# Sizes of the key and query weights from products of each weight chunk with itself on TensorE, and new instruction orders for the front of the kernel

## The chip, the cores and the metric

One core of a Trainium2 chip runs the whole kernel in one launch. The metric is the device time of one execution in microseconds (us); the kernel before took 1075.58 us, the median of 3 runs (1073.62 to 1076.91). Five engines work side by side, each in the order of its own instruction list, and wait for each other by semaphores: PE (TensorE, matrix products), DVE (VectorE), ACT (ScalarE), POOL (GpSimd) and SP (SyncE, which here only issues DMAs).

## The reference

The kernel is one transformer block with adaptive layer norm: linear attention with 32 heads, then a feed-forward layer with SiLU. There are 2048 tokens of width 576; the hidden width is 4608.

```python
mod = (_silu(c) @ w_mod).reshape(c.shape[0], 6, 1, -1)
sa, ca, ga, sb, cb, gb = (mod[:, 0], mod[:, 1], mod[:, 2], mod[:, 3], mod[:, 4], mod[:, 5])
h = _layernorm(x, axis=-1) * (1 + ca) + sa
x = x + ga * _A_ref(h, A_wqkv, A_wo)     # qkv = h @ wqkv; phi(t) = (t+1 if t>0 else exp(t)) + 1e-6
                                         # num = phi(q) @ (phi(k)^T v); den = phi(q) . sum phi(k); (num/den) @ wo
h = _layernorm(x, axis=-1) * (1 + cb) + sb
x = x + gb * _B_ref(h, B_w1, B_w2)       # silu(h @ w1) @ w2
```

Nothing in the reference is a norm of a weight. The norms are the kernel's own: it needs a power of two for each matrix that brings it into the range of 16-bit floats.

## The kernel before, in words

**Numbers.** TensorE multiplies 16-bit floats. Each 32-bit operand is scaled by a power of two and split into a high part (its value rounded to 16 bits) and a low part (the remainder); a product is three passes, high by high, low by high and high by low. The power of two for the key weights and for the query weights comes out of `find_size` (L514): from a bound of the matrix's norm it takes the square root's exponent by shifting the bits of the float (`scale_bits`, L511) and makes five small columns from it, SIZE, INV and the three of BY.

**How the work is tiled.** Tokens stand in 16 tiles of 128 rows, four tiles to a block. The width of 576 is cut in five chunks (START = 0..4): four of 128 and a tail of 64, which is loaded twice, into rows 0 to 63 and 64 to 127. The arrays `acc[0]` to `acc[15]`, 128 x 576 each, later hold the results; at the start they serve as landing places: `acc[0..4]` for the five chunks of the key weights, `acc[5..9]` for those of the query weights, `acc[12..15]` for the second block of x.

**The front of the kernel**, which the change touches, runs like this (the lines are those of the kernel before):

- SP issues the loads: two tiles of x, four full chunks and one tail of the modulation weights `w_mod` (`hT` and `tmod` in the profile), the key weights, two more tiles of x, the second block of x, the query weights.
- DVE and POOL normalise the first tiles (L367 to L384). ACT squares and sums the rows of `w_mod` (L626, L627). From their norm and that of the condition vector comes ETA, the power of two of the modulation (L628 to L639). DVE sums up four weighted chunks of `w_mod` (L645 to L654) and PE turns them into columns of shift and scale (`mod_col_of`, L563), which `add_cols` (L567) puts in `col_a`.
- **Key size.** For each key chunk DVE reduces the absolute maximum of every row (L641). The five maxima are squared and multiplied by 576 (L642), summed (L516), summed over the partitions by a product with a matrix of ones (L517), and turned into the scale (L518 to L527).
- With it the key weights are split: ACT makes the high parts (L500), DVE (L507) or POOL (L508, L509) the low parts.
- The first two tiles, turned by PE (L573), are modulated and split (L669, L392, L276), and PE multiplies them by the key weights into two banks of PSUM, `psK` (L590).
- **Query size.** ACT squares each query chunk with a sum over the row (L680, five times, each followed by a read of the accumulator). `find_size` then does the same as for the keys, and the query weights are split by L500, L507, L508, L509.
- `sigma_steps` (L968) makes the scale of the transformed keys. It uses the five maxima of the key size again: copied and multiplied in (L975, L977), reduced with two other rows (L978), summed by PE (L981), multiplied (L985).
- Then `phi` on each product: ACT takes the exponential (L530), DVE the linear part (L533) and the minimum with the sum (L542). The products with the query weights of tile 0 and 1 follow in the same two `psK` banks (L938), then keys and queries in turn for all tiles, and the sums over tokens of x^T phi(k) (L1087, `psG`).

`keep_busy` (L584) multiplies the matrix of ones by itself into a spare room, so that PE is never long without work in the front.

**After that** come the small matrices of all heads, the output projection (L420), the scales and first groups of the feed-forward layer (L1540, L1551), and from about 345 us to the end the feed-forward layer itself, which alternates products up (L2035) and down (L2119).

**What sets the order.** The instructions are first written in the order of the code and of a planner (tables STAGE_A and the class `Schedule`, the same before and after). At the end `arrange(ORDERS, begun)` lays a written permutation over the list of each engine: the table `ORDERS` names, by number, which instruction follows which. An engine never starts an instruction before the one ahead of it in that list.

## Time and profile before

| | |
|---|---|
| median of 3 runs | 1075.58 us (1073.62 to 1076.91) |
| the profiled execution | 1071.29 us |
| its span, first to last instruction | 1069.4 us |
| PE busy | 1042.4 us, 97% of the span |
| DVE busy | 901.8 us, 84% |
| ACT busy | 726.4 us, 68% |
| POOL busy | 753.2 us, 70% |
| mean granted clock of PE | 0.990 |

The profile is one execution. "Busy" counts an instruction from its start to its end, also while it is held up inside. A group's row gives the line, the engine, output and input, the shapes and the count, then busy us and the mean ns of one, then the idle time of the engine just before it and who ended it. A timeline row gives start, length, engine, line and operation. A product of two 32-bit operands has two records of PE in the timeline (x28 is 14 products). In the windows each row gives the length, the busy time and count of each engine, the granted clock of PE (1.00 is full speed), the DMA share and GB/s.

### The profile page before, as it was taken

The page shows a single profiled execution, that of the slowest core. Times are in us where ns is not written, and L with a number is a line of the kernel's source. Part 1 is how long each engine was busy: PE and PEld are TensorE (multiplying, and loading weights), DVE is VectorE, ACT ScalarE, POOL GpSimd, SP SyncE. Part 2 cuts the span into 40 slices and gives each one's busy share as a digit, 9 for nine tenths or more (in the row PEclk, how much of TensorE's full clock was granted, in tenths as well). Part 3 has the DMA queues.
Part 4 walks back from the last instruction along what each step waited for, and adds up shares of the span by engine and source line. Part 5 has one row for each costly group of instructions (what it writes and reads, how often), then busy time and mean ns, then how long its engine had stood idle before and what let it go on. Part 6 is the DMA issues. An engine that isn't in the chain of part 4 may idle for free.

```text
span 1069.4 us, 19132 instructions
## 1 busy us (share of the span) xinstructions
PE 1042.4 (97%) x6999; PEld 698.5 (65%) x6999; DVE 901.8 (84%) x1495; ACT 726.4 (68%) x1350; POOL 753.2 (70%) x818
## 2 busy tenths in 40 slices
PE   6889999999999999999999999999999999999998
PEld 5667778877776555666666666666666666666665
DVE  6998886698999999998988888977977987898767
ACT  5787585338667886776767767767767766676554
POOL 2586637466843888789798678876877778677563
PEclk7899999999999999999999999999999999999999
DMA  9299983096666877487667667667576667626423
GB/s 285 81 247 181 110 225 85 11 207 181 153 184 226 246 252 230 120 311 207 180 215 210 188 214 215 190 216 208 172 221 207 201 181 249 190 77 200 164 80 111
DMA packets 139245, 198.74 MB, mean 186 GB/s; under 512 B 63820, under 2 KB 96464, under 8 KB 139152
## 3 DMA queue, kind: packets, MB, share of 16 engines
q1 hardware_dynamic: 106340, 196.35, 61.5%
q10 hardware_dynamic: 32812, 1.18, 3.0%
q8 instruction: 54, 0.88, 0.3%
q14 instruction: 39, 0.32, 0.1%
HBM read 176.77 MB, written 15.48 MB: 180 GB/s over the span
## 4 chain that ended last, share of the span: by engine, by line
PE 81%; DVE 12%; DMA 3%; issue 1%; ACT 1%; SPq 1%; POOL 0%; DVEq 0%; ACTq 0%; POOLq 0%
PE up L2035 34%; PE down L2119 31%; PE psK L938 6%; PE psG L1087 5%; PE big L1551 1%; DVE st L367 1%; PE big L420 1%; DMA acc<-in_A_wqkv_dram 1%; PE small L1540 1%; DVE pn L810 1%; DVE hT L276 1%; DVE acc L1479 1%; DMA tmod<-in_w_mod_dram 1%; DMA hT<-hd 1%; PE down L2153 1%
## 5 line engine op out<-in xcount | busy, mean ns | idle before, releaser
L2035 PE MATMUL up<-hT,w 128*128 128x512 f16 x1264 | 320.0, 379 | 0.2 <-DMA hT<-hd 0.2
L2035 PEld LDWEIGHTS <-w 128*128 128x128 f16 x1492 | 145.9, 98 | 132.8 <-issue 1.5
L2128 DVE SCALAR_TENSOR_TENSOR acc<-acc,set,down 128x576 f32<-128x576 f32 x128 | 103.4, 809 | 31.2 <-PE down L2119 30.4
L2053 ACT ACTIVATE f<-f,set 128x512 f32<-128x512 f32 x102 | 73.2, 719 | 61.1 <-DVE f L2059 54.4
L2073 POOL TENSOR_TENSOR s<-f,f 128x256 f32<-128x256 f32 x66 | 54.7, 828 | 72.6 <-ACT f L2054 70.2
L2119 PE MATMUL down<-w,hc 128*128 128x288 f16 x600 | 91.8, 286 | 0.2 <-DVE acc L2128 0.2
L2119 PE MATMUL down<-w,hb 128*128 128x288 f16 x600 | 91.6, 286 | 0.0
L2057 DVE TENSOR_TENSOR f<-up,p 128x512 f32<-128x512 f32 x102 | 69.7, 683 | 18.0 <-PE up L2035 11.2
L2119 PE MATMUL down<-w,hT 128*128 128x288 f16 x480 | 82.7, 286 | 0.1
L938 PEld LDWEIGHTS <-hT 128*128 128x128 f16 x700 | 68.2, 98 | 21.2 <-issue 2.8
L2054 ACT ACTIVATE f<-f,set 128x512 f32<-128x512 f32 x102 | 73.6, 722 | 3.1
L2119 PEld LDWEIGHTS <-hb 128*128 128x128 f16 x600 | 58.7, 98 | 22.6 <-issue 0.2
L2119 PEld LDWEIGHTS <-hc 128*128 128x128 f16 x600 | 58.7, 98 | 22.2 <-issue 0.5
L2097 POOL TENSOR_TENSOR hc<-s,hc 128x512 f16<-128x512 f32 x50 | 63.8, 1275 | 6.1 <-ACT hc L2093 6.1
L420 PE MATMUL big<-w,qT 128*128 128x288 f16 x448 | 66.4, 286 | 1.6 <-DVE acc L1479 1.4
L2077 POOL TENSOR_TENSOR f<-f,s 128x256 f32<-128x256 f32 x66 | 53.5, 811 | 18.5 <-DVE hb L2097 10.2
L1087 PE MATMUL psG<-w,xs 128*128 128x288 f16 x448 | 64.6, 286 | 1.9 <-DVE w L966 1.5
L2059 DVE TENSOR_TENSOR f<-up,f 128x512 f32<-128x512 f32 x68 | 46.7, 687 | 23.0 <-PE up L2035 22.3
L2119 PEld LDWEIGHTS <-hT 128*128 128x128 f16 x480 | 47.0, 98 | 26.1 <-issue 0.3
L2070 POOL TENSOR_TENSOR s<-f 128x256 f32<-128x256 f32 x66 | 56.6, 857 | 7.9 <-ACT f L2050 3.8
L2075 POOL TENSOR_TENSOR s<-s,f 128x256 f32<-128x256 f32 x66 | 55.8, 845 | 3.3
L2119 PE MATMUL down<-w,ha 128*128 128x288 f16 x396 | 56.4, 286 | 0.0
(465 smaller groups left out, 2721.8 us busy)
## 6 DMA issues: line engine op xcount, KB each, us to landing
hT<-hd SPq DMA_DIRECT2D x101, 640.0 KB, 4.6
hT<-hd SPq DMA_DIRECT2D x65, 512.0 KB, 4.2
hT<-in_B_w_dram SPq DMA_DIRECT2D x14, 576.0 KB, 5.2
hT<-in_B_w_dram SPq DMA_DIRECT2D x28, 256.0 KB, 6.4
raw<-in_B_w_dram SPq DMA_DIRECT2D x11, 576.0 KB, 6.3
v<-in_B_w_dram SPq DMA_DIRECT2D x9, 576.0 KB, 5.8
acc<-in_A_x_dram SPq DMA_DIRECT2D x16, 288.0 KB, 4.8
raw<-in_B_w_dram SPq DMA_DIRECT2D x9, 512.0 KB, 5.8
```

The source lines that it names most:

```text
L420: T.matmul(ps, xpart(a), wpart(b), start=n == 0, stop=n == len(XW) - 1)
L938: T.matmul(o, part(a), w(b), start=c == 0 and m == 0, stop=c == KC and m == 1)
L1087: T.matmul(ps[:, h, :HALF], l, pk[pp[t]][:, u, h * HALF : (h + 1) * HALF], start=t == 0 and m == 0, stop=t == 3 and m == len(left) - 1)
L2035: T.matmul(ps, left, right, start=first and m == 0, stop=m == len(seq) - 1, skip_group_check=True)
L2053: A.activation(f, f, AF.Silu, scale=factor(self.g, "inv"))
L2054: A.activation(f, f, AF.Identity, scale=factor(self.g, "delta"))
L2057: V.tensor_add(f, self.bank[bank[1]], self.p1)
L2070: G.tensor_sub(self.s3, half(i, 0, 0), half(i, 0, 1))
L2075: G.tensor_sub(self.s[:, 1:2], self.s[:, 0:1], half(i, 0, 0))
L2097: eng.tensor_sub(t[:, :, 1, :], src, t[:, :, 0, :])
L2119: T.matmul(ps[:, p, :HALF], left[:, u, p * P : (p + 1) * P], right[:, v], start=n in (1, 5, 7, 6) and j == 0, stop=j == len(passes) - 1, s ...
L2128: V.scalar_tensor_tensor(dst, dst, factor(self.g, "ratio"), ps[:, :, :HALF], op0=ALU.mult, op1=ALU.add)
```

## The change

1. `find_size` no longer gets row maxima or sums of squares. A new function `gram` lets PE multiply each 128-column piece of a weight chunk by itself, in 32 bits, and adds all 25 products of a matrix up in one 128 x 128 place of PSUM. DVE reduces the absolute maximum of each row of that place, and the rest of `find_size` goes as before. The five DVE reductions of the key weights (L641), their squaring (L642) and the sum (L516), and the five ACT passes over the query weights with their accumulator reads (L680) are gone; 50 products of PE in 32 bits (40 of 128 x 128 and 10 of 64 x 64) and two DVE reductions of 128 x 128 out of PSUM come in.
2. `sigma_steps` uses the key size's own bound, kept in `phis[:, 7:8]`, in place of the five maxima: L975 and L977 are gone, L978 reduces two rows and not three, L981 has two columns and not three, and the copy L984 and the product L985 become one multiplication.
3. Six `keep_busy` products are left out, and an unused memset (`eps`).
4. `ORDERS` is a new table. The instructions of DVE differ in order up to the 497th of 1497, of ACT up to the 296th of 1295, of POOL up to the 156th of 823, of SP up to the 150th of 477, and of PE over the first 4000 of 13550 (weight loads counted), which is up to about 345 us in the trace. Behind that the lists are the same but for a few rows of PE. SP now loads, in this order: a tile of x, the tail of `w_mod` in two parts around the second tile of x, the four full chunks of `w_mod`, the four full key chunks, tiles 2 and 3 of x, the key tail, the second block of x, the query tail and the four query chunks. Before, the key tail and two tiles of x stood elsewhere: the tail between the chunks of `w_mod`, the tiles behind the last key chunk.

```diff
-    def find_size(rows, spot, size, inv, by):
-        t, q = both_sizes[:, 0:1], both_sizes[:, 1:2]
-        V.tensor_reduce(t, rows, axis=AX.X, op=ALU.add)
-        T.matmul(psT()[:, spot : spot + 1], ones, t, start=True, stop=True, skip_group_check=True)
-        V.tensor_scalar(q, psT()[:, spot : spot + 1], 2.0**-80, None, op0=ALU.max)
-        scale_bits(q)
+    def gram(j, k):
+        full, at_ = acc[5 * j + k][: P if k < KC else 64], psT()[:, P + j * P : 2 * P + j * P]
+        for c in START:
+            y = full[:, c * P : min((c + 1) * P, D)]
+            n = y.shape[1]
+            T.matmul(at_[:n, :n], y, y, start=k == 0 and c == 0, stop=k == KC and c == KC, skip_group_check=True)
+
+    def find_size(j, size, inv, by):
+        t, q, at_ = both_sizes[:, 0:1], both_sizes[:, 1:2], psT()[:, 66 + j : 67 + j]
+        fw = phis[:, 7:8] if j == 0 else q
+        V.tensor_reduce(t, psT()[:, P + j * P : 2 * P + j * P], axis=AX.X, op=ALU.max, apply_absolute_value=True)
+        T.matmul(at_, ones, t, start=True, stop=True, skip_group_check=True)
+        V.tensor_scalar(fw, at_, 2.0**-80, None, op0=ALU.max)
+        scale_bits(q, fw)
...
     for k in START:
-        V.tensor_reduce(rows2[:, k : k + 1], acc[k], axis=AX.X, op=ALU.max, apply_absolute_value=True)
-    V.scalar_tensor_tensor(rows2, rows2, float(D), rows2, op0=ALU.mult, op1=ALU.mult)
-    find_size(rows2, 66, SIZE_K, INV_K, BY_K)
+        gram(0, k)
+    find_size(0, SIZE_K, INV_K, BY_K)
...
-    keep_busy(4)
+    keep_busy(2)
...
     for k in START:
-        A.activation(e_, acc[5 + k], AF.Square, accum_out=rows_q[:, k : k + 1])
-    find_size(rows_q, 67, SIZE_Q, INV_Q, BY_Q)
+        gram(1, k)
+    find_size(1, SIZE_Q, INV_Q, BY_Q)
...
             V.tensor_mul(u[:, 0], c1, c1)
-            V.tensor_mul(u[:, 0], u[:, 0], rows2)
             V.tensor_mul(u[:, 1], c0, c0)
-            V.tensor_copy(u[:, 2], rows2)
-            V.tensor_reduce(t3, u, axis=AX.X, op=ALU.add)
+            V.tensor_reduce(t3[:, 0:2], u[:, 0:2], axis=AX.X, op=ALU.add)
...
-            V.tensor_copy(t3, ps)
-            V.tensor_mul(t3[:, 1:2], t3[:, 1:2], t3[:, 2:3])
+            V.tensor_scalar(t3[:, 0:2], ps, phis[:, 7:8], None, op0=ALU.mult)
...
         "DVE": """
-            0 16-17 7 6 1-2 10 9 8 11-14 42 15 43-44 29-30 28 46 26 18 5 4 27 31 19 32 45 20-21 33 22 34-36 23 84 38
```

The rows of the lists name line, operation, output and input, and shape; lines behind about L510 stand 6 to 8 lower in the kernel after.

**PE, where the key size is made.** Before, PE multiplies the columns of the modulation and the sums of the two sizes one behind the other:

```order
L563 MATMUL psG_123<-ones,hT 128x1 x5
L573 MATMUL psG_124<-ident,xt 128x128
L631 MATMUL psG_124<-crow,ones 128x2
L517 MATMUL psG_124<-crow,ones 128x1
L563 MATMUL psG_123<-sc,hT 128x1
L563 MATMUL psG_123<-plus_86,hT 128x1
```

After, the products of the key chunks (`acc_90`, then the tail in `acc_91`) stand behind the sum for ETA (now L638); this is the beginning of them:

```order
L571 MATMUL psG_122<-ones,hT 128x1 x5
L571 MATMUL psG_122<-sc,hT 128x1
L638 MATMUL psG_123<-crow,ones 128x2
L571 MATMUL psG_122<-plus_86,hT 128x1
L519 MATMUL psG_123<-acc_90 128x128 x4
L519 MATMUL psG_123<-acc_90 64x64
```

and this their end, with the sum of the key size (L525):

```order
L519 MATMUL psG_123<-acc_91 128x128 x4
L519 MATMUL psG_123<-acc_91 64x64
L571 MATMUL psG_122<-sc,hT 128x1
L571 MATMUL psG_122<-plus_86,hT 128x1
L525 MATMUL psG_123<-crow,ones 128x1
```

So the key size now stands behind 25 products on PE, and these behind the product that waits for the squares of `w_mod`. The 25 products of the query weights stand likewise ahead of all but four of the first products with the key weights (L598, L590 before).

**DVE, around the key size.** Before, the list goes from the last row maximum (L641) through the key size (L516 to L521), and normalises and modulates behind it:

```order
L641 TENSOR_REDUCE crow<-acc_91 128x1
L642 SCALAR_TENSOR_TENSOR crow<-crow 128x5
L632 COPY crow<-psG_124 128x2
L516 TENSOR_REDUCE crow<-crow 128x1
L654 SCALAR_TENSOR_TENSOR hT<-hT,sc 128x256
L634 TENSOR_SCALAR crow<-crow 128x1
L512 TENSOR_SCALAR crow<-crow 128x1
L518 TENSOR_SCALAR crow<-psG_124 128x1
```

After, the statistics of tiles 2 and 3 (BN), the first column of `col_a` and the first modulated piece stand ahead of the key size, whose reduction is L524:

```order
L645 TENSOR_SCALAR crow<-plus_86,crow 128x2
L367 BN_STATS st<-xt 128x6
L575 SCALAR_TENSOR_TENSOR col_a<-psG_122,crow 128x2
L367 BN_STATS st<-xt 128x6
L368 BN_AGGR mv<-st 128x2
L372 TENSOR_SCALAR mv<-mv 128x2
L702 TENSOR_TENSOR xs_112<-xt,xs_112 128x64
L392 TENSOR_SCALAR raw_127<-psK,col_a 128x256
L524 TENSOR_REDUCE crow<-psG_123 128x1
L526 TENSOR_SCALAR phis<-psG_123 128x1
```

What moved ahead of the key size is work that does not need it; the two low parts of the key weights that DVE makes (L507) moved the other way, behind the query size.

**DVE, where tile 3 of the keys is split.** Before, eight statistics of the third block stand ahead of the low part of the transformed keys (`w<-a,crow,w`, L966):

```order
L1012 TENSOR_TENSOR xs_118<-xt,xs_118 128x64
L367 BN_STATS st<-acc_94 128x6 x4
L368 BN_AGGR mv<-st 128x2 x2
L367 BN_STATS st<-acc_94 128x6 x4
L368 BN_AGGR mv<-st 128x2 x2
L533 TENSOR_SCALAR acc_91<-psK,phis 128x576
L392 TENSOR_SCALAR acc_93<-acc_93,col_a 128x512
L1040 TENSOR_SCALAR mv<-mv 128x4
L966 SCALAR_TENSOR_TENSOR w<-a,crow,w 128x576
```

After, the low part (now L972) comes first:

```order
L541 TENSOR_SCALAR a<-psK,phis 128x576
L550 SCALAR_TENSOR_TENSOR a<-z,phis,a 128x576
L392 TENSOR_SCALAR acc_92<-acc_92,col_a 128x512
L541 TENSOR_SCALAR acc_90<-psK,phis 128x576
L972 SCALAR_TENSOR_TENSOR w<-a,crow,w 128x576
L367 BN_STATS st<-acc_93 128x6 x3
L368 BN_AGGR mv<-st 128x2
```

The statistics moved behind it.

More of the change, by code (lines that the diff above doesn't have):

```diff
@@ new lines @@
+            1125-1132 1007-1010 987-990 1011-1014 991-994 1161-1164 1133-1138 1165-1166 995-996 1139-1140 1015-1018
+            1141-1148 997-998 1149-1154 1167-1170 1019-1020 1155-1156 1171-1178 1157-1160 1179-1180 1190-1191
+            1181-1186 1192-1193 1187-1188 999-1000 1194-1209 1240 1210-1213 1001-1002 1241-1242 1238-1239 1003-1004
+            1243-1244 1250-1255 1340-1341 1256-1257 1189 1258-1259 1342-1343 1214-1235 1260-1265 1236-1237 1266-1273
+            1344-1345 1274-1295 1245 1296-1314 1346-1347 1315-1317 1246-1247 1318 1248-1249 1319-1320 1348-1349
@@ new lines @@
+            1321-1338 1350-1368 1339 1369-1429 1442-1445 1470-1471 1446-1447 1430-1431 1472-1473 1448-1451 1432-1437
+            1452-1453 1438-1441 1474-1483 1454-1457 1484-1491 1458-1461 1492-1497 1462-1467 1498-1499 1468-1469
+            1500-1519 1526-1529 1554-1555 1520-1521 1556-1561 1522-1523 1562-1563 1524-1525 1564-1573 1530-1541
+            1574-1581 1542-1553 1582-1607 1610-1617 1608-1609 1618-1623 1638-1639 1624-1631 1640-1645 1632-1633
+            1646-1649 1682-1683 1634-1637 1666 1670-1671 1667 1672-1673 1668-1669 1684-1685 1650-1655 1686-1691
@@ new lines @@
+            1846-1853 1884-1885 1854-1855 1829 1856-1859 1886 1830-1831 1887-1888 1832-1833 1889-1890 1834-1837
+            1891-1893 1860-1863 1870-1872 1864-1865 1873 1894-1897 1874-1875 1898-1903 1876-1877 1904-1913 1926
+            1914-1915 1922 1878 1927 1978 1879-1881 1979 1923 1916-1917 1924 1928-1929 1918-1919 1925 1930-1933
+            1938-1943 1980 1920-1921 1981-1983 1944-1945 1934 1946-1949 1935 1950-1959 1966-1969 1936 1970 1992-1995
+            1937 1996-1998 1960-1961 1971-1973 1984-1985 1974-1975 1962-1965 1976 1999-2000 2006-2009 2001-2002 1977
@@ new lines @@
+            2572-2573 2522-2527 2536-2539 2580-2581 2540-2541 2582-2587 2548-2553 2560-2561 2594-2599 2574-2579
+            2606-2612 2600-2602 2562-2565 2603 2613 2620-2627 2588-2589 2604 2590-2593 2634-2635 2605 2636-2639
+            2614-2619 2628-2632 2646-2651 2633 2640-2645 2658-2662 2652 2663-2664 2653 2665 2654-2657 2672-2679 2726
+            2680-2682 2666-2667 2683-2685 2668-2671 2686-2697 2727 2706 2728 2698-2702 2707 2703-2705 2729 2708
+            2712-2719 2709 2720-2725 2710-2711 2744-2745 2730-2731 2746-2749 2732-2740 2750-2755 2741-2742 2756
@@ L201 @@
+            194-195 201 196 198-199 179 200 202 204 207 189 209 205 181 208 212-213 215 210 191 203 216 211 214 206
+            190
         """,
@@ L300 @@
     plus1 = const.tile([P, 2], F32, name="plus1")
-    eps = const.tile([P, 1], F32, name="eps")
     bc = {n: pool.tile([P, D], F32, name=f"bc_{n}") for n, pool in (("ga", pa), ("gb", const))}
@@ L974, in terms @@
             V.tensor_mul(u[:, 0], c1, c1)
-            V.tensor_mul(u[:, 0], u[:, 0], rows2)
             V.tensor_mul(u[:, 1], c0, c0)
-            V.tensor_copy(u[:, 2], rows2)
-            V.tensor_reduce(t3, u, axis=AX.X, op=ALU.add)
+            V.tensor_reduce(t3[:, 0:2], u[:, 0:2], axis=AX.X, op=ALU.add)
         do("DVE", 0.4, terms, [], ["some"])
-        pe(0.25, lambda: T.matmul(ps, ones, t3, start=True, stop=True, skip_group_check=True), ["some"], [g])
+        pe(0.25, lambda: T.matmul(ps, ones, t3[:, 0:2], start=True, stop=True, skip_group_check=True), ["some"], [g])
         def scale():
-            V.tensor_copy(t3, ps)
-            V.tensor_mul(t3[:, 1:2], t3[:, 1:2], t3[:, 2:3])
+            V.tensor_scalar(t3[:, 0:2], ps, phis[:, 7:8], None, op0=ALU.mult)
             V.scalar_tensor_tensor(t3[:, 0:1], t3[:, 0:1], 4.0 * D * XBY**2, t3[:, 1:2], op0=ALU.mult, op1=ALU.add)
```

235 lines of the change are left out of this document (107 added, 128 removed).

## The prediction

> **What bounds the kernel now.** I read the engines' busy time in stretches of 20 us first (length, then PE, PEld, DVE, ACT and POOL busy, the granted clock, DMA):
>
> ```profile
> 0.00:20.00 20.00, 12.57 (x69) 11.42 (x69) 10.31 (x23) 11.84 (x23) 4.95 (x11) 0.80 0.91 260
> 20.00:40.00 20.00, 13.65 (x78) 12.73 (x78) 19.16 (x69) 12.91 (x27) 10.49 (x9) 0.69 0.43 140
> 40.00:60.00 20.00, 17.50 (x140) 13.50 (x138) 18.40 (x41) 18.38 (x29) 12.48 (x10) 1.00 0.58 169
> 60.00:80.00 20.00, 17.86 (x144) 13.81 (x142) 19.53 (x28) 16.56 (x24) 14.90 (x11) 1.00 1.01 250
> 80.00:100.00 20.00, 19.44 (x158) 15.08 (x157) 19.53 (x25) 14.73 (x21) 13.97 (x9) 1.00 1.02 147
> 100.00:120.00 20.00, 20.00 (x166) 15.98 (x164) 14.31 (x30) 14.07 (x20) 13.80 (x10) 1.00 0.63 189
> ```
>
> From 100 us PE is full, so there the time is PE's work, which the change leaves alone. In front of that DVE is full, from about 20 to 100 us (19.16, 18.40, 19.53, 19.53), and PE is not; much of its busy time up to 40 us is the idle work of L584. What the front takes is then added to the whole. The chain of waits says the same: DMA, then almost only DVE, until PE takes over at 56.35.
>
> ```profile
> 9.22 9.18 DMA acc<-in_A_wqkv_dram
> ...
> 55.52 0.76 DVE acc L533
> 56.35 5.55 PE psK L938 x44
> ```
>
> So the question is how much sooner than 55.44 (the timeline's start of that L533) DVE gets to it.
>
> **The change part by part.** Gone are these two groups:
>
> ```profile
> L641 DVE TENSOR_REDUCE crow<-acc 128x1 f32<-128x576 f32 x5 | 3.6, 744 | 0.7 <-DMA acc<-in_A_wqkv_dram 0.7
> L680 ACT ACTIVATE e<-acc 128x576 f32<-128x576 f32 x5 | 3.4, 672 | 0.0
> ```
>
> The 3.6 us of DVE are worth less than they look: they ran in 16.3 to 21 us, partly while DVE waited for the chunks themselves. The ACT squares were not waited for at all; ACT then sat idle until the query size:
>
> ```profile
> 17.74 1.16 ACT L626 ACTIVATE acc<-hT 128x1152 f32<-128x1152 f32 x1 [2.06 <-DMA hT<-in_w_mod_dram]
> 22.88 0.78 ACT L500 ACTIVATE w<-acc,crow 128x576 f16<-128x576 f32 x1 [2.94 <-DVE crow L521]
> 40.22 2.11 ACT L500 ACTIVATE wq<-acc,crow 128x576 f16<-128x576 f32 x3 [1.85 <-DVE crow L521]
> 45.72 0.83 ACT L530 ACTIVATE e<-psK,phis,crow 128x576 f32<-128x576 f32 x1 [1.31 <-PE psK L590]
> ```
>
> So what counts is when the sizes are known, and what DVE does between. The rows of DVE for it:
>
> ```profile
> 22.12 0.16 DVE L518 TENSOR_SCALAR crow<-psG 128x1 f32<-128x1 f32 x1
> 23.89 1.07 DVE L977 COPY crow<-crow 128x5 f32<-128x5 f32 x1
> 27.57 0.81 DVE L507 SCALAR_TENSOR_TENSOR w<-acc,crow,w 128x576 f16<-128x576 f32 x1
> 33.26 1.12 DVE L507 SCALAR_TENSOR_TENSOR w<-acc,crow,w 128x576 f16<-128x576 f32 x1
> 38.38 0.15 DVE L516 TENSOR_REDUCE crow<-crow 128x1 f32<-128x5 f32 x1
> 39.44 0.16 DVE L518 TENSOR_SCALAR crow<-psG 128x1 f32<-128x1 f32 x1 [0.46 <-PE psG L517]
> 42.61 1.12 DVE L975 TENSOR_TENSOR crow<-crow 128x5 f32<-128x5 f32 x1
> 44.61 0.48 DVE L985 TENSOR_TENSOR crow<-crow 128x1 f32<-128x1 f32 x1
> 46.59 0.88 DVE L533 TENSOR_SCALAR a<-psK,phis 128x576 f32<-128x576 f32 x1 [0.28 <-ACT e L530]
> 47.38 0.75 DVE L1010 TENSOR_TENSOR xs<-xt,xs 128x512 f16<-128x512 f32 x1
> 55.44 0.83 DVE L533 TENSOR_SCALAR acc<-psK,phis 128x576 f32<-128x576 f32 x1
> ```
>
> *Price of a product.* The nearest rows are L584's, the same shape and type, and the clock beside them:
>
> ```profile
> 28.56 5.17 PE L584 MATMUL psG<-ones 128*128 128x128 f32 x28
> 33.57 0.41 PE L590 MATMUL psK<-w,hT 128*128 128x288 f16 x2
> ...
> 38.46 0.83 PE L584 MATMUL psG<-ones 128*128 128x128 f32 x6
> 39.12 0.28 PE L517 MATMUL psG<-crow,ones 128*128 128x1 f32 x2
> ```
> ```profile
> 28.00:30.00 2.00, 2.00 (x11) 2.00 (x11) 1.96 (x4) 2.00 (x5) 2.00 (x2) 0.50 0.19 64
> 30.00:32.00 2.00, 2.00 (x11) 2.00 (x11) 1.97 (x7) 0.28 (x2) 1.92 (x3) 0.50 0.00 0
> 32.00:34.00 2.00, 1.98 (x16) 1.66 (x15) 2.00 (x5) 1.43 (x3) 1.76 (x2) 0.91 0.00 0
> ```
>
> At full clock three products take 39.12 - 38.46 = 0.66, so 0.22 each. The run of 28 records (14 products) began at 28.56 and the clock rose at about 32.2 (0.91 of a window of 2 us), 3.6 us later; its last 1.4 us held some 6 products, so the other 8 took 3.6, 0.45 each. A chunk is four such products and one of 64 x 64, taken as half: 1.0 us at full clock, 2.0 at half; a matrix 5 or 10.
>
> *Step 1, the key size comes later.* The new order of SP loads `w_mod` whole, then four key chunks, two tiles of x, then the key tail. Counted by sizes (576 KB for each of four chunks of `w_mod`, 288 KB for a full chunk of keys or a tile of x, 144 KB for each half tail), that is 3.2 MB to the end of `w_mod` and 5.3 MB to the end of the key tail. At the 260 GB/s of the first row above these are 12.5 and 20.4 us; I take 14 and 20, as the rate is lower at first. ACT's squares of the last chunk and of the tail are 1.3 and 0.9 us (L626's row with its read; L627 has half its columns): 16.6. Behind them PE forms the sum for ETA, and then starts on the keys, at 17.6. It has then had work for about 0.4 us; by the 3.6 us just read the clock rises at 20.9. Until then 1.7 chunks, then 3.3: done at 24.3 (bounds 22.6 and 27.6, all at full and all at half clock). The DVE reduction of 128 columns (0.744 for 576; some 0.25), the sum and two waits make 0.8: the size is read at 25.1, against 22.12. That is **3.0 later**, and DVE has nothing to do for some 4 us before it.
>
> *Step 2, DVE from the key size to the query size.* Before 38.38 - 22.12 = 16.3. Moved ahead of the key size, into the idle 4 us: four statistics of 0.4 (1.6), the rest of ETA and small work (0.7), a column, a modulation, and two aggregates (1.0). Gone: L977 (1.0). Moved behind: two L507 (1.8). Added from later: one modulation and one subtraction (0.9). 16.3 - 1.6 - 0.7 - 1.0 - 1.0 - 1.8 + 0.9 = 11.1, so DVE is there at 36.2. PE must have done the query products: they follow four key products that need the first ACT split (two L500 and a modulation after 25.7, so 27.6) and the loads, which were all in before 30 (64 GB/s in 28 to 30, then 0); about 29 + 5 = 34 (39 at half clock). DVE decides, and the size is read at 37.0 against 39.44: **2.4 sooner**.
>
> *Step 3, from there to the first phi.* Before 46.59 - 39.44 = 7.15. Gone: L975 and L985, 1.5. Added: the two L507 (1.6) and L1010 from behind (0.75). 8.0, so 45.0. PE's way is as long: 52 products of keys at 0.12 (20 us for 166 of them in the last row of the first view) and ten transposes at the 0.22 of a product, 8.5 after 36.9; tile 0 is ready about 1.2 ahead of that, at 44.2, and the exponential (0.83) makes 45.0. I take 45.1: **1.5 sooner**. ACT's table load, moved from 6 us to behind the third chunk, lies in ACT's wait for the query size (before 1.85 and five squares long).
>
> *Step 4, to the L533 that PE waits for.* Before 55.44 - 46.59 = 8.85; less L1010 (0.8), plus small steps of the key scale that now stand ahead (0.4): 8.45, so 53.5, **1.9 sooner**.
>
> *Step 5, a wait behind it.*
>
> ```profile
> PE psG L1087 <- DVE w L966: 1.5, 1, 1.5
> ```
>
> The low part L966 now stands ahead of the eight statistics, so this wait should go; other work of DVE is late in its place, so I take 1.0 of 1.5 (bounds 0 and 1.5).
>
> *Step 6, 100 to 345 us.* The order is new there too, but PE's waits are small:
>
> ```profile
> PE big L420 <- DVE acc L1479: 1.4, 2, 1.1
> PE up L2035 <- DVE acc L1556: 0.5, 1, 0.5
> ```
>
> With the smaller rows of the same view (five of 0.2 to 0.4) they are some 3.5 in all: the most that can be won; a new order can as well add as much. I take 0, bounds -2 and +2.
>
> *Sum:* -1.9 - 1.0 + 0 = **-2.9**. The profiled execution took 1071.29 with a span of 1069.4; it would take 1068.4. The median of the runs is 4.3 above that execution, and 1075.58 - 2.9 = **1072.7**. The fewer L584 products weigh nothing, as they fill PE's idle time.
>
> **The rivals.**
>
> *The saved stalls go elsewhere.* L977 and L975 take 1.07 and 1.12 for five columns, where their like take 0.15, and both start beside a product of POOL:
>
> ```profile
> 23.79 1.14 POOL L508 TENSOR_TENSOR acc<-acc,crow 64x576 f32<-64x576 f32 x1 [6.42 <-issue]
> 42.40 1.31 POOL L508 TENSOR_TENSOR acc<-acc,crow 128x576 f32<-128x576 f32 x1 [3.08 <-ACT wq L500]
> ```
>
> They ended when it did, so they had waited for it. POOL keeps its ten such products, so the next DVE instruction of that kind may wait in their stead: 0.9 back in step 2 and 1.0 in step 3. Then -1.0, 1074.6. Against it: most of the rows that come next read PSUM or are statistics, and the same trace has those beside POOL at their usual length.
>
> [...]
>
> *More than that.* PE's clock is up from the first key chunk (22.6 and not 24.3), and a third of the waits behind 100 us goes too: -2.9 - 1.7 - 1.0 = -5.6, 1070.0. For it: PE is at work from 14 us on the columns; against it: before, such work ran from 16 us on, and the clock still stood at half in 28 to 30.
>
> *PE cold.* All key chunks run at half clock: 27.6 and not 24.3, +3.3, and the sum is +0.4, 1076.0. For it: the 3.6 us could be longer where PE's work has gaps, and it waits for the chunks.
>
> [...]
>
> *Slower: the key tail is late.* It is issued behind two tiles of x, and the second block of x right behind it. Transfers in flight together share the engines: the last chunk of `w_mod` and the last key chunk landed at 17.7 and 18.4, although issued apart. If the tail lands with the last of the loads, at 28.5, PE has cooled: 2.0 for the chunk and 0.8 to the read, 31.3, which is 6.2 more than step 1: +3.3, 1078.9. It turns the sign from a landing at about 26.2. Against it: the queue before gave the key chunks within 18.4 with as many bytes queued behind them.
>
> **How the numbers follow.** The forecast (-5 to -0.8 as its own range, by the clock in step 1 and the bounds of 5 and 6) gets 0.50, more than that 0.20, the stalls moved on 0.10, PE cold 0.12, the late tail 0.08. About 0.3%, 3.2 us, is what a measurement of this kernel can tell from no change. Faster by over that: 0.44 of the forecast's chance (0.22) and all of the larger gain, 0.42. Slower: the late tail, and 0.05 of the cold PE with a bad order behind, 0.13. The same: 0.45. The range goes from 1069.2 to 1077.4; it leaves out the late tail and the end of the larger gain.
>
> **What would show it.** Right: the ACT split of the keys begins at 25 to 26, later than 22.88, and the query's at 37 to 38, sooner than 40.22; PE's full stream (L944, L938 before) starts its pass after the first query phi at about 54.4 and not 56.3; the wait for the low part of tile 3 is gone; DVE idles some 4 us before the key size. Wrong: a key size at 28 or later; DVE instructions of 1 us on few columns as many as before; PE waits of over 4 us in all between 100 and 345; or a PE that is not full there. And if PE's work behind 345 us were not as long as before, the whole reckoning would miss its ground.

## The result, and the profile after

The kernel after takes **1078.22 us** (median of 8 runs, 1077.58 to 1085.42); the kernel before, beside it, 1073.26 (8 runs, 1070.53 to 1076.91). The ratio is 1.0063, with a 95% interval of 1.0036 to 1.0089: **0.6% slower**. Run again later against 29 runs of before, it gave 1.0065 (1.0044 to 1.0086); one of its 12 runs, of 2237.02 us, was slow and is left out of that. The forecast was 1072.7, in a range to 1077.4, so the sign and the range both missed. The 1075.58 that the forecast started from was the median of three runs; against the 1073.26 of all eight, the change cost 5.0 us where a gain of 2.9 was forecast.

The profiled execution of after took 1078.32 with a span of 1076.6, against 1071.29 and 1069.4. The same stretches as in the prediction (length, then busy us of PE, PEld, DVE, ACT and POOL, the granted clock, DMA share and GB/s), with one more row behind them:

```profile
0.00:20.00 20.00, 17.52 (x90) 16.49 (x91) 11.17 (x37) 10.42 (x22) 3.68 (x9) 0.94 0.92 294
20.00:40.00 20.00, 18.49 (x129) 16.22 (x128) 12.81 (x43) 10.97 (x19) 9.24 (x9) 0.89 0.40 113
40.00:60.00 20.00, 16.20 (x125) 12.41 (x125) 17.04 (x41) 17.19 (x27) 12.15 (x10) 1.00 0.43 130
60.00:80.00 20.00, 19.32 (x157) 15.30 (x157) 17.29 (x20) 16.23 (x23) 17.10 (x12) 1.00 0.93 287
80.00:100.00 20.00, 19.83 (x161) 15.30 (x160) 17.37 (x30) 16.30 (x23) 11.92 (x8) 1.00 1.15 102
100.00:120.00 20.00, 17.34 (x139) 13.36 (x138) 12.14 (x22) 13.03 (x19) 12.81 (x9) 1.00 0.78 196
120.00:360.00 240.00, 235.83 (x1767) 176.89 (x1765) 207.25 (x371) 144.66 (x239) 132.61 (x117) 1.00 0.65 154
```

The change did to DVE what it was to do: 12.81 us busy in 20 to 40 and not 19.16. PE took over as the busy engine there (18.49, before 13.65). But in 100 to 120, where PE had been full, it is now idle for 2.66 us. DVE's timeline in the front, with the key size (its second L526 is the query size), the first phi and the L541 that PE's full stream waits for:

```profile
25.31 0.29 DVE L524 TENSOR_REDUCE crow<-psG 128x1 f32<-128x128 f32 x1 [4.12 <-PE psG L519]
26.07 0.16 DVE L526 TENSOR_SCALAR phis<-psG 128x1 f32<-128x1 f32 x1 [0.47 <-PE psG L525]
...
40.38 0.29 DVE L524 TENSOR_REDUCE crow<-psG 128x1 f32<-128x128 f32 x1 [2.13 <-PE psG L519]
...
41.15 0.16 DVE L526 TENSOR_SCALAR crow<-psG 128x1 f32<-128x1 f32 x1 [0.41 <-PE psG L525]
...
49.10 0.88 DVE L541 TENSOR_SCALAR a<-psK,phis 128x576 f32<-128x576 f32 x1 [0.39 <-ACT e L538]
...
59.09 0.88 DVE L541 TENSOR_SCALAR acc<-psK,phis 128x576 f32<-128x576 f32 x1
```

| step | before | predicted | after |
|---|---|---|---|
| key size read | 22.12 | 25.1 | 26.07 |
| query size read | 39.44 | 37.0 | 41.15 |
| first phi | 46.59 | 45.1 | 49.10 |
| L533 (after: L541) that PE waits for | 55.44 | 53.5 | 59.09 |

So the front is 3.65 us later and not 1.9 sooner. PE's timeline tells what the query size waited for:

```profile
16.92 8.35 PE L519 MATMUL psG<-acc 128*128 128x128 f32 x50
...
31.43 1.65 PE L592 MATMUL psG<-ones 128*128 128x128 f32 x6 [1.24 <-DVE raw L392]
32.87 7.47 PE L519 MATMUL psG<-acc 128*128 128x128 f32 x50
```

The 25 query products ran behind the warming products (L592, `keep_busy`), from 32.87 to 40.34; DVE had ended its last instruction at 38.26 and then sat idle for 2.13. Further on, PE's idle time in 100 to 120 leads back to one load. The chain of waits in that stretch and the timelines of ACT, DVE and PE:

```profile
95.94 4.72 DMA turned<-acc
...
101.16 10.90 DMA raw<-in_w_mod_dram
112.06 0.02 issue
112.08 1.26 ACT raw L1145
113.33 0.71 ACT acc L390
114.04 0.72 ACT e L538
```
```profile
112.08 1.26 ACT L1145 ACTIVATE raw<-raw,sc 64x1152 f32<-64x1152 f32 x1 [4.94 <-DMA raw<-in_w_mod_dram]
...
114.87 0.88 DVE L541 TENSOR_SCALAR acc<-psK,phis 128x576 f32<-128x576 f32 x1 [3.00 <-ACT e L538]
...
116.46 0.41 PE L1090 MATMUL psG<-w,xs 128*128 128x288 f16 x2 [1.59 <-DVE sum L1100]
```

ACT stood for 4.94 us at a tail of the modulation weights for the feed-forward half, which nobody needs soon; behind it in its list stood the exponential (L538) that DVE's L541 waits for; L1100, which PE waits for, is DVE's next instruction. In the kernel before SP had issued this load 22 us sooner, and ACT did not wait:

```profile
79.15 0.48 SPq L465 DMA_DIRECT2D raw<-in_w_mod_dram  x1
...
105.12 1.25 ACT L1142 ACTIVATE raw<-raw,sc 64x1152 f32<-64x1152 f32 x1
```

Where the 7.2 us of span went can be read as a lag: how much later the same instruction starts than before (the median over the instructions of DVE, ACT and POOL around a time). It is about 1.8 at 100 us (the 3.65 less 1.85 of idle time that PE no longer has in 60 to 100), 4.5 at 130, 5 to 6 up to 360, 7 at 400 and 7.3 at the end.

### The profile page after: what moved, and what is told of

It is laid out like the page before. It is cut to its first block, busy times and chain, and to the rows that moved or that the text cites. A ratio compares the mean times of both kernels' runs of the same rounds, so it can differ in the third digit from the quotient of the medians.

```text
span 1076.6 us, 19301 instructions
## 1 busy us (share of the span) xinstructions
PE 1055.8 (98%) x7087; PEld 708.6 (66%) x7087; DVE 899.0 (84%) x1485; ACT 722.6 (67%) x1340; POOL 753.0 (70%) x818
## 4 chain that ended last, share of the span: by engine, by line
PE 79%; DVE 9%; DMA 5%; ACT 3%; issue 2%; POOL 1%; SPq 1%; DVEq 0%; POOLq 0%; ACTq 0%
PE up L2038 32%; PE down L2122 30%; PE psK L944 4%; PE psG L1090 3%; PE big L420 2%; PE psG L519 1%; PE big L1554 1%; DMA hT<-hd 1%; DMA raw<-in_w_mod_dram 1%; DMA acc<-in_A_x_dram 1%; DVE st L367 1%; DMA turned<-acc 1%; PE psK L1301 1%; DVE hT L277 1%; PE small L1543 1%
## 5 line engine op out<-in xcount | busy, mean ns | idle before, releaser
L1090 PE MATMUL psG<-w,xs 128*128 128x288 f16 x448 | 67.6, 286 | 1.8 <-DVE sum L1100 1.6
L944 PE MATMUL psK<-w,hT 128*128 128x288 f16 x392 | 56.1, 286 | 2.7 <-DVE acc L541 1.5
```

Source lines behind the costliest of these rows:

```text
L944: T.matmul(o, part(a), w(b), start=c == 0 and m == 0, stop=c == KC and m == 1)
L1090: T.matmul(ps[:, h, :HALF], l, pk[pp[t]][:, u, h * HALF : (h + 1) * HALF], start=t == 0 and m == 0, stop=t == 3 and m == len(left) - 1)
```

## The experiments

Four causes were open, and the expectations set them against each other: the place and price of the products in the front (there Theory 1, and Theory P for the price); SP's order, which makes one load late (Theory 2); the new order behind the front (Theory 3); and the clock of PE in the front (Theory 4). "Warm" and "cold" stand for a granted clock of 1.00 and of 0.50. In the kernels built on after, line numbers stand up to five higher or one lower, since the table of orders is longer or shorter (L541 is L543, L542 or L546, L519 is L521, L520 or L518); in those built on before up to three. "Before" is always its runs beside the kernel.

**The two halves apart.** The new code with the order of before on all engines, and the code of before in the new order.

> The new statistics (50 products) with the old order of every engine: each instruction that both kernels have stands where it stood before, the key and the query products stand directly ahead of the product that sums their size. Theory 1: the products cost about 7.3 us of TensorE each, of which the key ones lie in an idle stretch and the query ones fill the 3.5 us wait that stood before the first key projections and push them 3 to 4 us later; 1076 to 1077.5. Theory 2 adds nothing here. Rival (the order alone makes the loss): 1073, as before.

> The old statistics (VectorE's maxima, ScalarE's squares) with the new order of every engine; the old instructions stand directly ahead of the size that they feed, or behind the ScalarE instruction that they followed. Theories 1 and 2: no product delays the front, the late load stays: 1073.3 plus 2.7 for the load, plus 1.5 behind 120 us, less 1.9 for the wait that the new order removes, 1075 to 1076. Rival (the order alone makes the loss): 1078 or more.

New code in the old order took 1090.06 (before 1073.62): ratio 1.0161 (1.0142 to 1.0179). Old code in the new order took 1084.44: 1.0101 (1.0082 to 1.012). The first missed both of its expectations; the second came out as its rival has it, at 1078 or more. Neither half explains the loss, since each is worse alone than both together. (How an old instruction is fitted into the other order was a choice, so these two runs don't price the halves.) In the first, DVE's old list has the key size ahead of the work on the first tiles, so that this work stands behind 25 products of PE:

```profile
20.00:30.00 10.00, 9.75 (x51) 8.47 (x51) 0.16 (x1) 0.00 (x0) 0.00 (x0) 0.65 0.69 230
```

For ten us three engines do nothing (0.16 of DVE, nothing of ACT and POOL) but wait for 50 records of PE:

```profile
20.39 9.76 PE L518 MATMUL psG<-acc 128*128 128x128 f32 x50 [0.25 <-DVE crow L638]
```

So it is the reorder that keeps the new statistics from costing more: 1.0161 without it, 1.0063 with it. In the second kernel the late load is there too (ACT waits 5.31 us for it), which puts that part on the order and not on the statistics.

**The late load.** In after, one SP issue, this tail of `w_mod`, goes ahead of the four writes `turned<-acc` and three more issues that were ahead of it:

```diff
 SP
+raw<-in_w_mod_dram          # entry 41 of the list
 turned<-acc x4              # entries 65 on
 ...
-raw<-in_w_mod_dram
```

> The changed kernel with one DMA issue moved in SyncE's queue: the load of the modulation weights that is issued at 101.16 us goes ahead of the four writes of turned rows (93.40), so it can be issued at about 91.8, when ScalarE has read its buffer. Theory 2 (late load): ScalarE's wait of 4.94 us at 112.08 is gone, and with it TensorE's waits at 100 to 120 us (1.6 us for the sum of line 1100 and 1.05 us for the cast of line 1032); the time falls by 2 to 2.7 us to about 1075.7. Rival: the turned rows, now behind the load, come later and TensorE waits as long for those; the time is 1077.5 or more.

1075.99 (1073.83 to 1082.04) against 1073.62: 1.0027 (1.0012 to 1.0042). The medians lie 2.2 below after, 3.6 below its second set of runs. The stretch and ACT's instruction:

```profile
100.00:120.00 20.00, 20.00 (x166) 15.97 (x164) 14.81 (x26) 14.15 (x20) 13.38 (x10) 1.00 0.65 191
```
```profile
107.39 1.26 ACT L1147 ACTIVATE raw<-raw,sc 64x1152 f32<-64x1152 f32 x1
```

PE is full again, and ACT's instruction has no wait in brackets behind it. This part of the loss is shown; it is about half of it.

**The start of the query products.** Their own wait is for DVE's L392 (here L394). In the program all of this lies in one PSUM tile of two banks: the products' place and the one that L394 reads are in different banks, but this program's waits go by tile, as the rows below show (1.24 us for L394). The first kernel drops the three warming products ahead of them (`keep_busy(3)`); the second also moves L394 ahead in DVE's list; the third moves the load as well.

```diff
-    keep_busy(3)
     k_part([0], [(0, KC)])
```
```diff
 DVE
 L577 SCALAR_TENSOR_TENSOR col_a<-psG_122,crow 128x4
+L394 TENSOR_SCALAR raw_128<-psG_123,col_a 128x256
 L670 TENSOR_SCALAR col_u<-col_a,crow 128x10
 L369 BN_STATS st<-acc_93 128x6 x2
-L394 TENSOR_SCALAR raw_128<-psG_123,col_a 128x256
```

> The changed kernel without the three warming products (of ones with ones) that stand in TensorE's queue between the first key products and the 25 query products; nothing else is moved. Theory 1 (place in TensorE's queue): the query products start at about 30.2 us of the span at full clock instead of 33.08 at half clock, end near 37.4 instead of 40.3, the query size is read about 3 us sooner than 41.15, the first feature sum that TensorE waits for (line 541, 59.09) comes 2 to 3 us sooner, and the time is 1075 to 1076 instead of 1078.2. Rival (the new order of the other engines sets the front): the query size comes sooner, the sum at 59.09 stays within 0.5 us, the time stays at 1078.

> The changed kernel without the three warming products ahead of the query products, and with VectorE's modulation of the last x chunk (line 392, raw out of psG, 30.85 us) moved up behind the columns that it reads (28.75), so that the query products do not wait for it. Theory 1 (the wait for that read, and the cold clock behind it, make the front late): the query products start near 30.2 us at full clock, take 7.3 us, end near 37.5; VectorE gets to their reduction at 38.3, the query size is read near 38.9 instead of 41.15, the sum at 59.09 comes 2 us sooner, the time is about 1076. Rival (work behind the query size sets the front): the size comes 2 us sooner, the sum at 59.09 stays within 0.5 us and the time stays at 1078.

> The edits of the run before in this table (query products not held up by line 392) and the modulation load moved ahead of the turned rows, together. If the late load and the late front are two separate causes, their gains add: 1078.2 less 2.2 for the load (measured) less about 2 for the front, 1074. If the front's gain is given back before 120 us, the time is that of the load's move alone, 1076.

| kernel | us (before) | ratio | query size | first phi | L541 |
|---|---|---|---|---|---|
| without the warming products | 1079.43 (1073.62) | 1.005 (1.003 to 1.007) | 40.60 | 48.54 | 58.53 |
| and DVE's read moved | 1080.58 (1073.91) | 1.0066 (1.0049 to 1.0083) | 38.96 | 48.57 | 58.11 |
| and the load moved | 1075.28 (1073.91) | 1.0012 (1.0002 to 1.0023) | 41.34 | 50.87 | 60.41 |

Without the warming products the query products themselves wait as long, and then run at half clock for the first part (the granted clock was 0.62 in 31.08 to 34.50 and 0.88 from there to 38):

```profile
31.45 8.35 PE L521 MATMUL psG<-acc 128*128 128x128 f32 x50 [1.24 <-DVE raw L394]
```

With DVE's read moved, they run at full clock throughout (6.80 us from 30.60 on, the clock at 1.00 from 30 to 38), and the query size is read 2.2 us sooner than in after. Yet the first phi comes only 0.5 sooner. PE's timeline of that kernel:

```profile
30.60 6.80 PE L521 MATMUL psG<-acc 128*128 128x128 f32 x50 [0.38 <-DVE raw L394]
...
38.54 0.38 PE L527 MATMUL psG<-crow,ones 128*128 128x1 f32 x2 [0.88 <-DVE crow L526]
...
40.15 2.51 PE L600 MATMUL psK<-w,hT 128*128 128x288 f16 x10
```

PE, done early, waits 0.88 for DVE's reduction; the granted clock is at half in 40 to 42 us (0.50), and ten projections take 2.51, where at full clock ten of this shape took 1.39 (after, at 60.02). From query size to first phi it takes 9.6 and not 7.95. And the whole gain of the front was then lost at the load (ACT waits 5.65 for it). With the load moved the time falls by 5.3 us. In this third kernel's profile the whole front is some 2.3 us late, from the key size on (28.39): its key products began at 18.29 and took 9.29. The second profile of after, whose key products took 6.80, the length at a clock of 1.00 in the second kernel, has both sizes 1.3 to 1.4 sooner than the first. So differences of that size between fronts can't be read from single profiles; the medians carry the verdicts.

**The query size without PE.** From the kernel with the load moved, the 25 query products are taken out, and ACT's five squares make the size as before.

```diff
 ...
-    for k in START:
-        gram(1, k)
+    for k in (4, 3, 0, 1, 2):
+        A.activation(e_, acc[5 + k], AF.Square, accum_out=rows_q[:, k : k + 1])
```

> The changed kernel with the modulation load moved, its key size from products as it is, its query size from ScalarE's squares as before (two of the five squares in ScalarE's idle time ahead of 26.84 us, three behind 31.9 us); the 25 query products are gone. Theory 1 in its first form (the query products hold TensorE to 40.3 us and push the key projections): the key projections start 4 us sooner than 41.12, the query size is read about when it was (41 to 42 us), and the time falls from 1076.0 to 1073 or 1074. Rival (the query size sets the front, not TensorE's room): no change from 1076.

1076.67 (before 1073.07): 1.0026 (1.0015 to 1.0037), as with the products. The room that these took on PE was not the price:

```profile
37.51 0.47 PE L1365 MATMUL psG<-ident,xt 128*128 128x128 f32 x1 [4.34 <-DVE raw L394]
...
41.21 2.43 PE L603 MATMUL psK<-w,hT 128*128 128x288 f16 x10
```

PE waits 4.34 us for DVE, comes back at half clock (2.43 for ten projections, at full clock 1.39; 0.92 in 40 to 60 us), and L541 (here L546) starts at 59.10, as in after. With the products PE is late; without them it is cold.

**Cheaper products.** The products read only the upper 16 bits of the weights, so one pass in place of 32-bit arithmetic: 25 records of PE for a matrix and not 50. This leaves the lower 16 bits of each weight out of the two norms; everything else is computed as before. The second kernel has the load moved too.

```diff
-            y = full[:, c * P : min((c + 1) * P, D)]
+            y = full.bitcast(mybir.dt.bfloat16).rearrange("p (d a) -> p d a", a=2)[:, c * P : min((c + 1) * P, D), 1]
```

> The changed kernel with the 50 products taken of the upper 16 bits of each weight alone (as bfloat16), so that each product is one pass of TensorE; the statistics leave out the lower 16 bits. Order and everything else stay. Theory P (the price of the 32-bit products is what makes the front late): a matrix takes 2 to 3 us of TensorE instead of 7.3 to 8.4, the key size is read 1 to 3 us sooner than 26.07, the query size near 38.9 (VectorE gets there at 38.3), the key projections start about 4 us sooner than 41.12, and the time is 1074 to 1076. Rival (place and order alone): 1078.

> One-pass products and the modulation load moved, the new order everywhere else. One-pass products alone gave 1075.2 with about 1.5 us of waits left at 105 to 120 us; without these 1073.5 if the two add, 1075 if the load's wait had been hidden there.

1075.15 against 1073.91, 1.0016 (1.0003 to 1.0029); with the load moved 1072.73 against 1073.07, 1.0001 (0.999 to 1.0013). Each lies some 3 us below its like with 32-bit products (after, and the kernel with the load moved). The query size of the first of them:

```profile
32.27 3.75 PE L521 MATMUL psG<-acc 128*128 128x128 bf16 x25
...
37.26 0.16 DVE L528 TENSOR_SCALAR crow<-psG 128x1 f32<-128x1 f32 x1 [0.61 <-PE psG L527]
```
```profile
47.62 0.88 DVE L543 TENSOR_SCALAR a<-psK,phis 128x576 f32<-128x576 f32 x1 [0.89 <-ACT e L540]
```

That is the predicted size (37.0), 10.4 us ahead of the phi and not 8: the clock stood at half from 30 to 42 us here (0.50 in each 2 us), and ahead of that, from 23.65 on, twelve records of warming products took 2.91 us, in after 1.58.

**The wait for the low part.** In the kernel *before*, the low part L966 of tile 3 goes ahead of the second set of four statistics.

```diff
 DVE
 L367 BN_STATS st<-acc_94 128x6 x4
 L368 BN_AGGR mv<-st 128x2 x2
+L966 SCALAR_TENSOR_TENSOR w<-a,crow,w 128x576
 L367 BN_STATS st<-acc_94 128x6 x4
```

> The kernel before with one VectorE instruction moved: the low part of line 966 goes ahead of the second set of four row statistics, as it stands ahead of them in the changed kernel. If TensorE's wait of 1.5 us at 77.58 was worth something by itself: 1.0 to 1.5 us faster than before, 1072. Rival: the statistics, now later, hold up what follows, no change, 1073.5.

1074.34 against 1073.91: 1.0011 (1.0002 to 1.002). PE's wait of 1.48 us for L966 is gone from the profile, but a longer one has come, for the L533 that now stands behind it in DVE's list:

```profile
80.72 1.14 PE L938 MATMUL psK<-w,hT 128*128 128x288 f16 x8 [2.00 <-DVE acc L533]
```

By itself, in the order of before, this move wins nothing.

**The order behind the front.** The kernel with the load moved, in the new order up to the instructions of about 135 us and in the order of before behind them; then the same with the one-pass products (which leave out the lower 16 bits as above).

> The changed kernel with the modulation load moved (as measured alone: 1076.0), and on every engine the new order only as far as it had come by 135 us of the span; what is left then follows in the old order. Theory 3 (the new order behind 135 us has more waits of its own): the lag against the kernel before, 1.2 to 2 us at 130 to 160 us in the run of the load's move alone and 5.2 at the end, no longer grows; 1073 to 1074. Rival (the growth behind 135 us comes with the late front, whatever the order): 1076.

> The same with the products of the upper 16 bits alone (one pass each). If the three causes are separate (price of the products, late load, new order behind 135 us), their gains add: about 1071.5, faster than both kernels. If not, it is no faster than the better of the two runs that hold one of them, 1073 to 1075.

The first: 1074.71 (1071.21 to 1079.71) against 1073.07, 1.0014 (0.9999 to 1.003). Its lag against before stays between 0.1 and 1.0 us from 130 to 400 us; with the new order kept (the kernel with the load moved) it had grown from 1.9 to 4.8. The second: **1069.81 (1067.18 to 1070.8) against 1073.07, 0.9962 (0.9948 to 0.9975)**, 0.4% faster than the kernel before and 0.8% faster than after. It runs about 1 us ahead of before from 130 to 400 us, and PE is full where it was:

```profile
100.00:120.00 20.00, 20.00 (x165) 15.96 (x164) 14.93 (x31) 12.80 (x19) 13.51 (x9) 1.00 0.65 180
120.00:360.00 240.00, 236.30 (x1760) 176.16 (x1757) 201.93 (x372) 151.35 (x253) 137.80 (x125) 1.00 0.65 161
```

By ratios to before: after +0.63%, load moved +0.27%, old order behind +0.14%, one pass -0.38%. The old order behind was worth 1.3 us of median on the 32-bit kernel and 2.9 on the one-pass kernel. The intervals are about 0.15% to either side, so the first of these two is only likely; the second is outside them. The lags of all profiles say the same: from 130 to 400 us the lag grew by 1.2 to 3.1 us in each of the ten with the new order there, among them the one with the old code, and changed by -1.3 to +0.9 in the six with the order of before.

**Warmth.** In that fastest kernel, six warming products move from ahead of the modulation columns to behind them, so that DVE gets the columns sooner; then DVE's read is moved as above.

```diff
 PE
-L593 MATMUL psG_123<-ones 128x128 x6
 L572 MATMUL psG_122<-sc,hT 128x1
 ...
-L593 MATMUL psG_123<-ones 128x128 x2
+L593 MATMUL psG_123<-ones 128x128 x8
```

> The run with one-pass products, the load moved and the old order behind 135 us (1069.8), with six warming products (22.85 to 25.76 us there, at half clock) moved behind the column products of line 572 that stand after them. Theory 4 (the warming products in this place hold up the columns that VectorE waits 2.87 us for at 27.29, and TensorE then stays at half clock to 41): the columns come 1.5 to 2.5 us sooner, the warming products run in one piece of 3.5 us behind them, the clock is full before 35 us, the sum at 56.42 comes 1 to 2 us sooner, and the time is 1068 to 1069. Rival (the sizes alone matter, the clock's state in 20 to 41 us is hidden): no change, 1069.8.

> The same, and VectorE's modulation of the last x chunk (raw out of psG) moved up behind its columns, so that TensorE does not wait for it (0.76 us at 30.04 before this edit). Theory 4: another 0.5 us. Rival: no change against the run before it in this table.

1071.74 against 1073.08, 0.9984 (0.9972 to 0.9995), and 1073.86, 1.0001 (0.9989 to 1.0013). By their medians each is slower than the kernel it came from, though the intervals overlap a little; neither is faster. The last columns are done 1.9 us sooner, and the query products now take 2.48 and not 3.75. But then:

```profile
31.03 2.48 PE L520 MATMUL psG<-acc 128*128 128x128 bf16 x25
35.01 0.33 PE L1361 MATMUL psG<-ident,xt 128*128 128x128 f32 x1 [1.50 <-DVE raw L393]
36.81 0.59 PE L526 MATMUL psG<-crow,ones 128*128 128x1 f32 x2 [1.47 <-DVE crow L525]
...
38.84 2.61 PE L599 MATMUL psK<-w,hT 128*128 128x288 f16 x10
```

PE waits twice for DVE, and ten projections take 2.61, as in the first one-pass kernel at a clock of 0.50. L541 starts at 58.46; in the kernel it came from, at 56.42. So the theory that earlier columns would pull the front in falls.

**The kernel after once more,** to see how far single profiles differ.

> The changed kernel once more, on the chip of the two runs above, so that its distance to the kernel before and to them is measured side by side: 1077 to 1079 against 1073 to 1074.

1079.62 against 1073.08 (ratio above). Its profile has L541 at 57.70, 1.4 sooner than the first, and the same wait of ACT for the load (4.33).

## Why the prediction was wrong

The sum was -1.9 for the front, -1.0 for the wait behind it and 0 from 100 us on. Measured by the lag it was +3.65, -1.85 and +5.4. The first and the last failed, in steps 2 and 6.

**Step 1, the key size, came near its number, in part by luck.** Predicted 25.1 with DVE idle for some 4 us, measured 26.07 with 4.12. The products began at 16.92, 0.7 sooner than taken, and took 8.35 and not 6.7. The clock rose at 20.84 (predicted 20.9), but not for the reason given. The prediction had it at half because PE would have had work for 0.4 us only. PE was busy for 9.19 of the 9.38 us from 7.54 to 16.92 and the clock was full (1.00) when the products began; it fell at 17.43 and was at half (0.50) for 3.41 us. The price was mis-sized in one place. The 128-wide products cost what was taken: in after at full clock (1.00 in 21 to 25 us) their records start 0.112 us apart (21.38 to 22.05), two to a product, so 0.22. The 64-wide one of each chunk was taken as half of that, 0.11. A whole chunk takes 1.35 (21.17 to 22.51), which leaves 0.45 for it, with the changes to it and back. A matrix is 6.8 and not 5.0. The second profile of after, with its key products in 6.80, has the key size at 24.80, so the number itself is within the spread of single executions.

**Step 2 is the step that failed first.** It said that PE would be done at about 34 (39 at half clock), that DVE would be there at 36.2, and that "DVE decides". DVE was there at 38.26, but PE ended at 40.34. The prediction had PE's query products start when their loads and the first ACT splits allowed it, 29. It overlooked a wait: the warming products ahead of them, and they themselves, write into the PSUM tile that DVE's L392 still reads, and that ended at about 31.4. The warming products then ran at half clock (0.50 from 31.08 to 34.50), and the query products took 7.47 and not 5. The size, forecast 2.4 sooner, was read 1.7 later. The wait could be read from the program. What the runs add is that mending it is not enough: with DVE's read moved the query size came at 38.96, but PE then cooled (0.50 in 40 to 42 us) and gave most of it back. DVE itself took 12.2 us between the sizes and not 11.1; the rows for that are under step 4.

**Step 3 held where PE was warm.** From the query size to the first phi it took 7.95; predicted were 8.1 (37.0 to 45.1). In the six kernels where PE was at half clock behind a size that came sooner than in after, it took 9.6 to 11.9 (ten projections 2.43 to 2.61 us, at full clock 1.39); in the one-pass kernel with the load moved, with a clock of 0.91 in 34 to 36 us and 1.00 behind, 7.94 again.

**Step 4 was 1.5 short:** 9.99 and not 8.45. DVE's and POOL's rows of the stretch, behind one pair of rows from step 2:

```profile
31.44 1.26 DVE L980 TENSOR_TENSOR crow<-col_u 128x5 f32<-128x5 f32 x1
...
49.89 1.22 DVE L277 TENSOR_TENSOR hT<-raw,hT 128x256 f16<-128x256 f32 x1
...
53.74 0.89 DVE L277 TENSOR_TENSOR hT<-raw,hT 128x256 f16<-128x256 f32 x1
...
55.34 1.04 DVE L507 SCALAR_TENSOR_TENSOR v<-acc,crow,v 64x576 f16<-64x576 f32 x1
```
```profile
31.41 4.05 POOL L509 TENSOR_TENSOR w<-acc,w 64x576 f16<-64x576 f32 x3
...
49.67 1.16 POOL L1013 TENSOR_TENSOR xs<-xt,xs 128x512 f16<-128x512 f32 x1
...
53.55 0.79 POOL L966 COPY zsum<-a 128x576 f32<-128x576 f32 x1 [2.72 <-DVE a L550]
54.31 1.46 POOL L509 TENSOR_TENSOR wq<-acc,wq 128x576 f16<-128x576 f32 x1
55.73 1.93 POOL L1147 TENSOR_TENSOR tmod<-tmod,acc 128x576 f32<-128x576 f32 x1
```

L277 takes 0.42 when undisturbed (0.41 to 0.43 in six rows from 27.54 to 53.40). Its two long ones began beside a product of POOL or its copy and ended within 0.3 us of it; L507 is 0.2 longer than its usual 0.81. Together some 1.5. The same is seen in step 2: L980, five columns, took 1.26 beside POOL's L509, where the same product took 0.15 in the kernel before; that is as much as DVE's 1.1 there, which PE's later end hid. So the rival "the saved stalls go elsewhere", to which the prediction gave a chance of 0.10, took place beside the larger misses. No run took POOL's work away, so this stays a reading of the trace.

**Step 5 held in the kernel after, though not by that move alone.** The wait for tile 3's low part is gone, and PE's idle time in 60 to 100 fell from 2.7 to 0.85 (two rows of each kernel), so more than the 1.0 was won there, and the lag shrank from 3.65 to about 1.8. In the kernel before, the move by itself gave 1.0011, since the wait went to another instruction. The gain belongs to the new order of the stretch, not to the one term that the prediction named.

**Step 6 is the other step that failed.** It took 0, with bounds of -2 and +2, from PE's waits behind 100 us in the kernel *before*, "the most that can be won". It did not ask what the new order would make late. SP's list stood in the change, and step 1 counted its loads up to the key tail; the order behind 60 us, where one load of `w_mod` was moved behind four writes, was not looked at. That cost 2.7 in the lag (1.8 at 100 us, 4.5 at 130) and 2 to 5 us of time by the pairs with and without it (medians: after 2.2, with DVE's read moved 5.3, one pass 2.4). The new order behind 135 us costs another 1.3 to 2.9. Why that order is worse, instruction by instruction, stays open. Two of the prediction's own signs of being wrong came: PE's waits between 100 and 345 were 5.8 us in all, over the 4 that it named, and PE was not full there.

**The rivals.** The slower one, a late key tail, gave 1078.9, near the result, but by another way, so that is luck: the key products ran without a wait for it, and the sign of the front was decided later. (Its turning point of 26.2 belongs to a chunk at full clock; with the 2.0 of its own sum it is 25.2.) "PE cold" named the right danger in the wrong place: the key products ran cold for 3.41 us only, but the warming products and the first of the query products did too, and in the kernels with an earlier size the key projections. The larger gain's condition, key products at full clock throughout, was met in the second profile of after (6.80 us). The front was 1.4 us sooner with it (L541 at 57.70) and still 2.3 later than before, since PE and not DVE set the query size. The chances (faster 0.42, same 0.45, slower 0.13) went nearly all to how much the front would gain, and almost nothing to the new order of the 245 us behind it.

## What to carry to other kernels

A new order has to be read for every queue that it changes and as far as it changes it; for each load that moves back, name the instruction that waits for it and what stands behind that one on its engine. Work that is moved to an idle engine is not free where the engine is in the chain a little later: price it to its end, the clock included, and ask which tile its output shares with a reader. To win back such a change, undo its parts one at a time: here the cheaper product, one issue of SP and the old order behind the front turned +0.63% into -0.38%.

## What was not expected of the hardware

- **Being early came with a lower clock.** Where PE was done sooner it waited for DVE, and the next stretch ran at half clock. Two kernels that differ in three warming products and one place in DVE's list: size at 41.15 and phi 7.95 later (1.00 in 40 to 60 us), size at 38.96 and phi 9.61 later (0.50 in 40 to 42). In after the granted clock changed at 17.43, 20.84, 31.08 and 34.50, so 3.41, 10.24 and 3.42 us apart; in the kernel before at 11.87 and 32.34, 20.47 apart. That is 1, 3, 1 and 6 times 3.41.
- **What lowers the clock stays open.** In the fastest kernel PE was 9.15 us busy in 20 to 30 and 9.75 in 30 to 40, and yet the clock was at half, from about 17.4 to 41.3:

```profile
20.00:30.00 10.00, 9.15 (x42) 8.03 (x40) 6.21 (x25) 4.92 (x10) 6.62 (x7) 0.50 0.69 199
30.00:40.00 10.00, 9.75 (x50) 7.10 (x51) 8.24 (x31) 8.37 (x13) 4.27 (x4) 0.50 0.20 60
```

  In after the same stretches, with 9.73 and 8.76 us busy, had 0.96 and 0.83. In after the clock fell at 17.43, although PE had been busy for 3.34 of the 3.41 us before that, and at 31.08 behind 2.25 of 3.41; in the kernel before it stayed full through two such stretches with 1.64 and 1.70 (32.34 to 39.17). Busy time as the profile counts it does not decide it alone; no run here settled what does.
- **A 64-wide product between 128-wide ones cost more than one of them, with the changes to it and back.** At full clock (after, 1.00 in 21 to 25 us) a chunk of four 128-wide products and a 64-wide one took 1.35 us in 32 bits, of which the four take 0.89, at 0.22 each, which leaves 0.45. In the tail chunk, with 64 rows and not 128, the 128-wide products took the same 0.22 (records 0.112 us apart, 24.07 to 24.74). All 25 together took 6.80 in 32 bits at a clock of 1.00; in one pass 3.75 at 0.50, and 2.48 in the kernel with the warming products moved.
